# Hash attention and a gated feed forward on one core: both halves of batch 0 taken pair of heads by pair of heads, and the feed forward one stage later

## The chip, the cores and the metric

The kernel runs on 1 core of one Trainium2 chip. The metric is the device time of one execution in microseconds (us). Three runs of the kernel before gave 350.76, 349.88 and 348.50 us; their median is 349.88. The profiled execution took 349.89 us, and the span of its trace, from the first to the last instruction, is 348.1 us.

## The reference

`q`, `k` and `v` have 4 batches, 8 heads, 768 tokens and 64 dimensions; `proj` is 64 x 6. A query attends only to keys with the same six sign bits. The result, 3072 tokens of 512, goes through an RMS norm and a gated feed forward of width 1536.

```python
q_bits = (einsum('bhsd,dk->bhsk', q, proj) > 0)
k_bits = (einsum('bhsd,dk->bhsk', k, proj) > 0)
mask = q_bucket[:, :, :, None] == k_bucket[:, :, None, :]
scores = where(mask, q @ k.T / sqrt(D), -1e9)
attn = softmax(scores)
x = (attn @ v)                      # laid out as [3072, 512]
xn = x / sqrt(mean(x * x) + 1e-6) * rms_g
g = xn @ w_gate
out = (silu(g) * (xn @ w_val)) @ w_out
```

## The kernel before

**Windows, stages, slots.** The 768 queries of a batch are cut into two halves of 384, so that there are eight windows w of one batch and one half each. For one window and one head the scores come in three parts of 256 keys: two matmuls fill a tile of PSUM (`scores`, L351), and one exponential of 128 x 768 on ScalarE (ACT) empties it into `psb` (`probs`, L361). One such part is a slot, and a stage is the 24 slots of a window. Batch 0's first window alone is cut again (`UNITS`, L32): a first unit of 128 queries with 8 slots, so that its feed forward can begin early, and a second of 256 with 16. There are 192 slots in all (`SLOTS`, L34).

**Masking by bits.** The bits of a query and a key are carried as 12 extra rows of the score matmul (`KROWS` = 76). For a head, q and k are turned so that the head's dimension lies on the partitions, kept in FP32 in `T0`, multiplied with `proj` (`hash_bank`, L219), turned into signs on VectorE (`signs`, L226, the tile `bits`) and moved into rows 64 to 75 of the FP16 tile `QK`. The moves are copies on VectorE (L258) or ACT (L250, L254), or DMAs on SyncE (SP): L263 and L264 for one head, L276 for two heads (`hash_heads`, eight DMAs), L293 for two pairs (`hash_two`, eight DMAs). The values are cast into `QK` by GpSimd (POOL), L179, L194 and L211.

**Two ways to turn.** For the pairs in `BY_PE` (L38; all four of batch 0, the first two of batch 1), whole rows are loaded in one DMA (`load_rows`, L108), TensorE (PE) transposes them (`turn_pe`, L167), and VectorE or ACT copies them out (`keep`, L175). For all other pairs the load is made of blocks (`load_blocks`, L118): four DMAs for k and four for q of a pair, in pieces of 128 bytes; VectorE then transposes 32 x 32 blocks (`turn_dve`, L203).

**After the scores.** Two steps after a head's last slot `av` (L375) multiplies `psb` with `v`; after a pair of heads `attn_out` (L391 and on) adds the mean of v, divides and writes `x`. There is a single PSUM tile for `av`, and two for scores. `norm` and `turn_x` make `xnT`. The feed forward of a unit is 12 pairs of `gate` (L470, four matmuls, Tanh on ACT) and `value` (L481, four matmuls, two products on VectorE), and `project` (L495) makes the three output chunks of a window, twelve matmuls of 512 columns each. These share three banks of PSUM.

**What sets the order.** The order is written by hand: `at(s, f, ...)` places a step behind slot s, ranks order the steps of a slot, and each engine then carries out its instructions strictly in that order. `work` (L612) holds the slots at which each pair of batches 1 to 3 is loaded (k, q, v) and turned. All loads, the bits' DMAs and the outputs go through SP's queue in the order of the program; an instruction of SP waits for its tile and for one of eight semaphores. The weights `wg`, `wv` and `wo` are loaded on POOL's queue in six halves, with a cast to FP16 on the way (L543, L549). Ten buffers hold raw loads.

**Timing of the feed forward.** From window 1 on, the feed forward of a window lies in slots 8 to 24 of the stage after its attention, and its projection in the nine slots after that. The first unit's feed forward lies in slots 13 to 24, the second's in 31 to 47. The weights are issued ahead of the loop and at slots 1, 3, 6 and 8. After the last slot come the last projection of window 6, the norm, feed forward and projection of window 7.

Of the kernel before, what the change touches and what calls it, by code (L numbers as in the profile page):

```python
# [41 lines left out]
def kernel(  # L42
# [99 lines left out]
    def q_cols(w, h, i0, ni):  # L142
        b, half = divmod(w, 2)
        t = QK[b, h // 2][0:KROWS, h % 2]
        if (b, h // 2) in BY_PE:
            o = half * S + HALF + i0
            return t[:, o : o + ni]
        if b == 1:
            return t[:, 0:S].rearrange("p (c e t) -> p e c t", e=2, t=128)[:, half]
        return t[:, half * HALF + i0 : half * HALF + i0 + ni]  # L150
# [4 lines left out]
    def out_chunk(w, c):  # L155
        b, half = divmod(w, 2)
        return 2 * c + half if b < 2 else 3 * half + c
# [25 lines left out]
    def turn_head(h, n=HALF, which="kq"):  # L183

        if "k" in which:
            keep(nc.vector, 0, h, "k")
            cast_half(0, h, "k", 0)
            cast_half(0, h, "k", 1)
        if "q" in which:
            ps = keep(nc.scalar, 0, h, "q")  # L190
            nc.scalar.copy(block(0, h, 1)[:, 0:n], ps[0:64, 0:n])

    def cast_rest(h):
        nc.gpsimd.tensor_copy(block(0, h, 1)[:, 128:], t0(0, h, "q")[0:64, 128:])  # L194
# [39 lines left out]
    late = {}  # L234
# [8 lines left out]
    def hash_head(h, n=HALF, k0=None, k1=None):  # L243
# [6 lines left out]
        nc.scalar.copy(bit_rows(0, h, 1)[:, 0:n], bt[32:44, 0:n])  # L250
        for eng, t in ((k0, 0), (k1, 2)):
            src = bt[32 * t : 32 * t + 12]
            if eng is nc.scalar:
                nc.scalar.copy(bit_rows(0, h, t), src)  # L254
            elif eng is nc.sync:
                nc.sync.dma_start(out=bit_rows(0, h, t), in_=src)
            else:
                nc.vector.tensor_copy(bit_rows(0, h, t), src)  # L258
        late[h] = bt

    def late_bits(h, n=HALF):
        if n < HALF:
            nc.sync.dma_start(out=bit_rows(0, h, 1)[:, n:], in_=late[h][32:44, n:])  # L263
        nc.sync.dma_start(out=bit_rows(0, h, 3), in_=late[h][96:108])  # L264

    def hash_heads(b, hp):
        ps = hash_bank(
            [(w[:, 0:32], t0(b, 2 * hp + hh, which))
             for hh in range(2) for w, which in ((pk, "k"), (pq, "q"))]
        )  # L270
        bt = bits_tile(hp)
        signs(bt, ps)
        for hh in range(2):
            for t in range(4):
                p0 = 64 * hh + 32 * (t % 2) + 12 * (t // 2)
                nc.sync.dma_start(  # L276
                    out=bit_rows(b, 2 * hp + hh, t), in_=bt[p0 : p0 + 12]
                )
# [31 lines left out]
    def v_mean(b, hp, n, parts=(None,)):  # L310
# [7 lines left out]
        if b == 0:  # L318
            nc.scalar.mul(cvb[b % 2][:, hs, 0:65], ps, C0 / S)
        else:  # L320
            nc.vector.tensor_scalar_mul(cvb[b % 2][:, hs, 0:65], ps, C0 / S)
# [5 lines left out]
    def score_parts(n, p):  # L327

        if n == 3:
            return [(2 * p + j, 0, HALF, j, 0) for j in range(2)]  # L330
        if n == 1:
            return [(jt, 0, 128, jt // 3, 128 * (jt % 3)) for jt in range(6)]
        return [(3 * p, 0, 256, 0, 0), (3 * p + 1, 0, 256, 1, 0),
                (3 * p + 2, 0, 128, 0, 256), (3 * p + 2, 128, 128, 1, 256)]

    def prob_at(n, jt, c):

        if n == 3:
            return jt // 2, jt % 2, 128 * c
        if n == 1:  # L340
            return 0, jt // 3, 128 * (jt % 3)
        p, m = divmod(jt, 3)
        return (p, m, 128 * c) if m < 2 else (p, c, 256)

    def scores(g):
        u, h, p = SLOTS[g]
        w, c0, n = UNITS[u]
        b = w // 2
        ps = scps.tile([128, 2, 512], FP32, name="s_ps")
        for jt, i0, ni, bk, col in score_parts(n, p):  # L350
            nc.tensor.matmul(  # L351
                ps[:, bk, col : col + ni], k_cols(b, h, jt), q_cols(w, h, 128 * c0 + i0, ni),
# [4 lines left out]
    def probs(g):  # L357
        u, h, p = SLOTS[g]
        if p == 0:
            psb[u, h] = ppool.tile([128, 3, 2, HALF], FP16, name="psb")  # L360
        nc.scalar.activation(  # L361
            psb[u, h][:, p], sps.pop(g)[:, :, 0:HALF], AF.Exp, scale=ESCALE,
        )

    def av(u, h, i0, i1):
        w, c0, n = UNITS[u]
        b = w // 2
        hp, hh = divmod(h, 2)
        if hh == 0 and i0 == 0:
            ot[u, hp] = ops.tile([128, 3, 2, 66], FP32, name="o_ps")  # L370
        o = ot[u, hp]
        for i in range(i0, i1):
            c, jt = divmod(i, 6)
            p, bk, col = prob_at(n, jt, c)
            nc.tensor.matmul(  # L375
                o[:, c, hh, 0:65],
                psb[u, h][:, p, bk, col : col + 128],
# [5 lines left out]
    def attn_out(u, hp):  # L383
        w, c0, n = UNITS[u]
# [4 lines left out]
        o = ot.pop((u, hp))  # L389
        tmp = spool.tile([128, 3, 2, 66], FP32, name="otmp")  # L390
        nc.vector.tensor_add(  # L391
            tmp[:, 0:n, :, 0:65], o[:, 0:n, :, 0:65],
            cvb[b % 2][:, 2 * hp : 2 * hp + 2, 0:65].unsqueeze(1).to_broadcast([128, n, 2, 65]),
        )
        r = spool.tile([128, 3, 2, 1], FP32, name="rcp")
        nc.vector.reciprocal(r[:, 0:n], tmp[:, 0:n, :, 64:65])  # L396
# [391 lines left out]
```

## Time and profile before

| what | us |
|---|---|
| device time, median of 3 runs | 349.88 |
| device time of the profiled execution | 349.89 |
| span of its trace | 348.1 |
| PE busy | 334.9 (96%) |
| VectorE busy | 238.2 (68%) |
| ACT busy | 216.7 (62%) |
| POOL busy | 138.6 (40%) |
| first exponential, slot 0 | 15.46 |
| slot 24 / slot 48 / slot 72 | 49.86 / 83.82 / 120.86 |
| end of the last exponential | 310.22 |
| mean granted clock of PE | 0.984 |

The table of the stages in the prediction has a row for each stretch between these slots. Matmuls are pipelined, so that a busy PE can stand for one that waits within its pipeline; the distance between the starts of two matmuls says more than their durations. In the trace some groups that the change touches are these (operation, out from in, shape and count, then busy us and mean ns of one, then idle time ahead of them and what ended it):

```profile
L361 ACT ACTIVATE psb<-s_ps 128x768 f16<-128x768 f32 x192 | 151.8, 809 | 26.6 <-PE s_ps L351 26.3
L203 DVE STREAM_TRANSPOSE kT<-kL 128x384 f32<-128x384 f32 x20 | 17.7, 883 | 0.0
L175 DVE COPY kT<-t_ps 128x384 f32<-128x384 f32 x12 | 6.6, 554 | 3.3 <-PE t_ps L167 3.2
L175 ACT COPY qT<-t_ps 128x384 f32<-128x384 f32 x12 | 5.8, 479 | 3.6 <-PE t_ps L167 3.6
L179 POOL CAST QK<-kT 64x384 f16<-64x384 f32 x24 | 12.0, 501 | 9.6 <-DVE kT L175 8.7
L211 POOL CAST QK<-kT 64x768 f16<-64x768 f32 x20 | 16.4, 820 | 17.9 <-DVE kT L203 11.6
```

### The profile page before, as it was taken

Reading aid. Unit: us, or ns where it says so; the run is one execution under the profiler, and the core shown is the slowest. Engines: PE = TensorE matmul, PEld = TensorE weight load, DVE = VectorE, ACT = ScalarE, POOL = GpSimd, SP = SyncE. Lnnn points to the kernel's source line nnn. Section 1 sums busy time; section 2 is a strip of 40 time slices with the busy share of each in tenths; the row PEclk is TensorE's granted clock in tenths of the full one; section 3 lists DMA queues with packets and bytes.
Section 4 is the critical chain, followed back from the end, with each engine's and each line's share of the span. In section 5 each row is a group of like instructions: output and inputs, shape, how many; then the busy total and the mean of one; then the engine's idle time right before and its main releaser. Section 6 shows DMA issues by size and latency. Waiting matters only on the chain.

```text
span 348.1 us, 8206 instructions
## 1 busy us (share of the span) xinstructions
PE 334.9 (96%) x3172; PEld 212.5 (61%) x3172; DVE 238.2 (68%) x541; ACT 216.7 (62%) x361; POOL 138.6 (40%) x220
## 2 busy tenths in 40 slices
PE   8897998999999999999999999999999999999995
PEld 5456886666666655665566656665566656665553
DVE  3784566688678955897678866897467555675860
ACT  2587687677567755766567756775576766742321
POOL 5476544777214751286126551385111111111000
PEclk9997799999999999999999999999999999999999
DMA  7999944273399005930376008600200010001002
GB/s 216 322 237 190 246 169 89 41 130 80 61 174 149 3 6 145 185 48 5 81 179 119 3 16 200 122 2 6 73 32 1 2 60 33 2 2 74 16 3 90
DMA packets 80199, 31.42 MB, mean 90 GB/s; under 512 B 65240, under 2 KB 77216, under 8 KB 80160
## 3 DMA queue, kind: packets, MB, share of 16 engines
q1 hardware_dynamic: 76176, 26.11, 32.1%
q0 software_dynamic: 3680, 4.72, 7.9%
q8 instruction: 25, 0.41, 0.5%
q14 instruction: 14, 0.11, 0.1%
q10 hardware_dynamic: 304, 0.07, 0.1%
HBM read 28.32 MB, written 6.29 MB: 99 GB/s over the span
## 4 chain that ended last, share of the span: by engine, by line
PE 82%; DVE 11%; issue 3%; ACT 2%; POOL 2%; DVEq 0%; POOLq 0%; ACTq 0%
PE g_ps L470 17%; PE v_ps L481 17%; PE s_ps L351 16%; PE y_ps L495 15%; PE o_ps L375 9%; PE d_ps L219 3%; DVE bits L226 2%; PE x_ps L453 2%; DVE otmp L391 1%; DVE QK L258 1%; DVE xn L445 1%; DVE kT L175 1%; PE y_ps L745 1%; PE m_ps L315 1%; DVE kT L203 1%
## 5 line engine op out<-in xcount | busy, mean ns | idle before, releaser
L361 ACT ACTIVATE psb<-s_ps 128x768 f16<-128x768 f32 x192 | 151.8, 809 | 26.6 <-PE s_ps L351 26.3
L351 PE MATMUL s_ps<-QK 76*128 76x384 f16 (+2 forms) x448 | 96.6, 310 | 0.7 <-ACT psb L361 0.2
L472 ACT ACTIVATE t<-g_ps 128x384 f32<-128x384 f32 (+2 forms) x108 | 49.2, 456 | 55.7 <-PE g_ps L470 54.7
L470 PE MATMUL g_ps<-xnT,wg 128*128 128x384 f16 (+2 forms) x432 | 80.6, 309 | 1.2 <-DVE xnT L454 0.8
L481 PE MATMUL v_ps<-xnT,wv 128*128 128x384 f16 (+2 forms) x432 | 80.6, 309 | 0.7 <-DVE a L483 0.6
L495 PE MATMUL y_ps<-wo,ht 128*128 128x512 f16 x276 | 69.1, 378 | 0.3
L483 DVE SCALAR_TENSOR_TENSOR a<-t,g_ps 128x384 f32<-128x384 f32 (+2 forms) x108 | 53.9, 499 | 21.5 <-ACT t L472 19.8
L375 PEld LDWEIGHTS <-psb 128*128 128x128 f16 x1152 | 52.9, 99 | 19.3 <-issue 5.3
L484 DVE SCALAR_TENSOR_TENSOR ht<-a,v_ps 128x384 f16<-128x384 f32 (+2 forms) x108 | 55.1, 510 | 13.1 <-PE v_ps L481 3.3
L375 PE MATMUL o_ps<-vl,psb 128*128 128x65 f16 x1152 | 58.7, 195 | 2.1 <-DVE otmp L391 1.8
L399 POOL TENSOR_TENSOR x<-otmp,rcp 128x384 f32<-128x384 f32 (+2 forms) x27 | 20.4, 756 | 99.7 <-DVE rcp L396 99.5
L351 PEld LDWEIGHTS <-QK 76*128 76x128 f16 x448 | 40.0, 101 | 25.2 <-issue 1.7
L470 PEld LDWEIGHTS <-wg 128*128 128x128 f16 x432 | 39.2, 97 | 24.1 <-issue 2.9
L481 PEld LDWEIGHTS <-wv 128*128 128x128 f16 x432 | 39.3, 98 | 22.7 <-issue 1.2
L495 PEld LDWEIGHTS <-ht 128*128 128x128 f16 x276 | 24.1, 97 | 20.9 <-issue 0.5
L502 ACT COPY ysb<-y_ps 128x512 f32<-128x512 f32 x23 | 13.5, 586 | 29.4 <-PE y_ps L495 29.1
L391 DVE TENSOR_TENSOR otmp<-o_ps,cvb 128x390 f32<-128x390 f32 (+2 forms) x36 | 18.5, 513 | 17.1 <-PE o_ps L375 14.7
L454 DVE TENSOR_TENSOR xnT<-x_ps,gcol 128x512 f16<-128x512 f16 x24 | 16.6, 691 | 12.7 <-PE x_ps L453 12.6
L211 POOL CAST QK<-kT 64x768 f16<-64x768 f32 x20 | 16.4, 820 | 17.9 <-DVE kT L203 11.6
L226 DVE TENSOR_SCALAR bits<-d_ps,thr,scl 128x384 f16<-128x384 f32 x20 | 13.2, 677 | 12.9 <-PE d_ps L219 12.7
L211 POOL CAST QK<-qT 64x768 f16<-64x768 f32 x20 | 16.4, 820 | 11.9 <-DVE qT L203 11.0
L413 POOL TENSOR_TENSOR sq<-x 128x384 f32<-128x384 f32 (+1 forms) x24 | 19.2, 800 | 1.9
(74 smaller groups left out, 281.6 us busy)
## 6 DMA issues: line engine op xcount, KB each, us to landing
vL<-in_v_dram SPq DMA_DIRECT2D x16, 384.0 KB
out_dram<-ysb SPq DMA_DIRECT2D x23, 256.0 KB
kL<-in_k_dram SPq DMA_DIRECT2D x40, 96.0 KB
qL<-in_q_dram SPq DMA_DIRECT2D x40, 96.0 KB
kL<-in_k_dram SPq DMA_DIRECT2D x5, 384.0 KB
qL<-in_q_dram SPq DMA_DIRECT2D x5, 384.0 KB
wg<-in_moe_w_gate_dram POOLq DMA_DIRECT2D x2, 768.0 KB, 10.6
wv<-in_moe_w_val_dram POOLq DMA_DIRECT2D x2, 768.0 KB, 8.9
```

The source lines that it names most:

```text
L211: nc.gpsimd.tensor_copy(QK[b, hp][0:64, hh, o : o + S], T0[b, hp, which][64 * hh : 64 * hh + 64, :])
L351: nc.tensor.matmul(ps[:, bk, col : col + ni], k_cols(b, h, jt), q_cols(w, h, 128 * c0 + i0, ni), start=True, stop=True,)
L361: nc.scalar.activation(psb[u, h][:, p], sps.pop(g)[:, :, 0:HALF], AF.Exp, scale=ESCALE,)
L375: nc.tensor.matmul(o[:, c, hh, 0:65], psb[u, h][:, p, bk, col : col + 128], vls[b % 2][:, h, v_chunk(b, h, jt), 0:65], start=(hh == 0 and ...
L391: nc.vector.tensor_add(tmp[:, 0:n, :, 0:65], o[:, 0:n, :, 0:65], cvb[b % 2][:, 2 * hp : 2 * hp + 2, 0:65].unsqueeze(1).to_broadcast([128, ...
L399: eng.tensor_mul(xd.rearrange("p c (h d) -> p c h d", h=2), tmp[:, 0:n, :, 0:64], r[:, 0:n].to_broadcast([128, n, 2, 64]),)
L470: nc.tensor.matmul(g, wg[:, kt, fs], xnT[w][:, kt, cs], start=(kt == 0), stop=(kt == 3))
L472: nc.scalar.activation(t, g, AF.Tanh, scale=0.5)
L481: nc.tensor.matmul(vv, wv[:, kt, fs], xnT[w][:, kt, cs], start=(kt == 0), stop=(kt == 3))
L483: nc.vector.scalar_tensor_tensor(out=a, in0=t, scalar=1.0, in1=g, op0=ALU.add, op1=ALU.mult)
L484: nc.vector.scalar_tensor_tensor(out=ht[w][:, ft, cs], in0=a, scalar=0.5, in1=vv, op0=ALU.mult, op1=ALU.mult)
L495: nc.tensor.matmul(y, ht[w][:, ft, c * 128 : (c + 1) * 128], wo[:, ft, :], start=(ft == 0), stop=(ft == NF - 1),)
```

## The change

The units are gone. The 48 slots of batch 0 go through the pairs of heads; for each pair first the one half's two heads, then the other half's. Batches 1 to 3 keep their order.

- `BY_PE` holds batch 0 alone: the first two pairs of batch 1 are loaded in blocks and turned by VectorE, and their bits come from `hash_two`. All loads of batch 1 are given earlier slots (from slot 9 on instead of 21).
- The heads of batch 0 are prepared later: only heads 0 and 1 ahead of the loop; heads 2 and 3 in slots 0 to 4, heads 4 and 5 in slots 6 to 13, heads 6 and 7 in slots 16 to 23. The bits of heads 4 to 7 are moved by `hash_heads`, eight DMAs on SP for a pair.
- The six weight loads are issued at slots 4, 11, 17, 23, 29 and 35.
- The feed forward of window w lies in slots 24w + 48 to 24w + 64 and its projection in the nine after that, so it comes one stage later than before. Those of windows 6 and 7 lie behind the last slot.
- `v_mean` of batch 0 leaves ACT for VectorE; `AHEAD`, the slot from which an exponential is placed behind the early steps of the slot before, is 3 instead of 24.

```diff
-UNITS = [(0, 0, 1), (0, 1, 2)] + [(w, 0, 3) for w in range(1, 8)]
-BASE = [0, 8] + [24 * w for w in range(1, 8)]
-SLOTS = [(u, h, p) for u, (_, _, n) in enumerate(UNITS) for h in range(H) for p in range(n)]
+SLOTS = [(w, 2 * hp + hh, p) for hp in range(H // 2) for w in range(2)
+         for hh in range(2) for p in range(3)]
+SLOTS += [(w, h, p) for w in range(2, 8) for h in range(H) for p in range(3)]
+LAST = {(w, h): g for g, (w, h, p) in enumerate(SLOTS) if p == 2}
-BY_PE = [(0, hp) for hp in range(4)] + [(1, 0), (1, 1)]
+BY_PE = [(0, hp) for hp in range(4)]
...
+    def hash_heads(hp):
...
+        for hh, t in [(0, 0), (0, 2), (0, 1), (1, 0), (1, 2), (1, 1), (0, 3), (1, 3)]:
+            p0 = 64 * hh + 32 * (t % 2) + 12 * (t // 2)
+            nc.sync.dma_start(out=bit_rows(0, 2 * hp + hh, t), in_=bt[p0 : p0 + 12])
...
+    turn_head(nc.vector, 0, "k")
+    casts(0, 0)
+    turn_head(nc.scalar, 0, "q", True)
     columns_of_proj()
+    turn_head(nc.vector, 1, "k")
+    casts(0, 2)
+    hash_head(0, (nc.vector, nc.scalar, nc.vector, nc.sync))
+    turn_head(nc.scalar, 1, "q", True)
     scores(0)
+    hash_head(1, (nc.vector, nc.scalar, nc.vector, nc.sync))
+    v_prep(0, 0)
...
+    for hp, turns in ((1, (0, 1, 2, 3)), (2, (6, 8, 10, 12)), (3, (16, 18, 20, 22))):
+        for i, s in enumerate(turns):
+            at(s, keep_pair, hp, i, nc.scalar if hp == 1 and i % 2 else nc.vector)
+            at(s + (hp > 1), casts, hp, i)
+    at(2, hash_head, 2, (nc.vector, nc.vector, nc.vector, nc.sync))
+    at(4, hash_head, 3, (nc.sync, nc.sync, nc.sync, nc.sync))
+    at(13, hash_heads, 2)
+    at(23, hash_heads, 3)
...
+    for i, s in enumerate((4, 11)):
+        at(s, load_w, (wg, wv)[i], (moe_w_gate, moe_w_val)[i], 0, 768)
+    for i, s in enumerate((17, 23)):
+        at(s, load_w, (wg, wv)[i], (moe_w_gate, moe_w_val)[i], 768, 1536)
+    at(29, load_wo, 0, 6)
+    at(35, load_wo, 6, 12)
...
-        (1, 0): ((21, 22, 23), (28, 29, 30, 31)), (1, 1): ((24, 25, 26), (33, 34, 35, 36)),
-        (1, 2): ((27, 30, 33), (35, 37, 39, 40)), (1, 3): ((32, 35, 39), (41, 43, 45, 47)),
+        (1, 0): ((9, 11, 14), (24, 26, 28, 30)), (1, 1): ((15, 18, 20), (31, 32, 34, 35)),
+        (1, 2): ((22, 25, 30), (37, 38, 40, 41)), (1, 3): ((28, 32, 36), (43, 47, 49, 51)),
...
+        s0 = 24 * w + 48
         seen = set()
         for ft in range(NF):
-            for f, s in ((g_step, s0 + (ns * ft) // NF),
-                         (v_step, s0 + (2 * ns * ft + ns) // (2 * NF))):
-                at(s, f, u, ft, rank=4 if s in seen else 2)
+            for f, s in ((g_step, s0 + 16 * ft // NF), (v_step, s0 + (32 * ft + 16) // (2 * NF))):
+                at(s, f, w, ft, rank=4 if s in seen else 2)
                 seen.add(s)
+        for i in range(9 if w < 7 else 6):
             c, j = divmod(i, 3)
+            at(s0 + 16 + i, project, w, c, 4 * j, 4 * j + 4, rank=1 if i == 8 else 3)
-    AHEAD = 24
+    AHEAD = 3
```

More of the change, by code (lines that the diff above doesn't have):

```diff
@@ L156, in out_chunk @@
         b, half = divmod(w, 2)
-        return 2 * c + half if b < 2 else 3 * half + c
+        return 2 * c + half if b == 0 else 3 * half + c
     def turn_pe(b, h, which):
@@ L181, in cast_half, with turn_head @@
         )
[L183 to L194, printed above, removed]
+    def turn_head(eng, h, which, direct=False):
+        ps = keep(eng, 0, h, which)
+        if direct:
+            nc.scalar.copy(block(0, h, 1), ps[0:64])
     def turn_dve(b, hp, which, part):
@@ L726 @@
             f()
-    for s in range(NS, NS + 13):
+    for s in range(NS, 24 * 10):
         for _, _, f in steps(s):
             f()
-    project(6, 0, 0, NF)
-    norm(8)
-    project(6, 1, 0, NF)
-    for c in range(3):
-        turn_x(8, c)
-        project(6, 2, 4 * c, 4 * c + 4)
-    for ft in range(NF):
-        value(8, ft, gate(8, ft))
-    for c in range(2):
-        project(7, c, 0, NF)
     y = bank("y_ps")
```

282 lines of the change are left out of this document (83 added, 199 removed).

## The prediction

> **What bounds the kernel now.** I read the busy rows, then the span cut at the exponentials that open each stage of 24 steps, then the costliest groups, then the DMA issues in order of time. One slot is one exponential (L361, 192 of them); slot 0 starts at 15.46 us, slot 48 at 83.82, slot 72 at 120.86, and slot 191 ends at 310.22. Columns below: stretch, its length, busy us of PE, PEld, DVE, ACT, POOL, then granted clock, DMA share, GB/s.
>
> ```profile
> 0.00:15.46 15.46, 12.68 (x98) 8.16 (x102) 7.52 (x35) 5.56 (x12) 7.69 (x29) 1.00 0.88 270
> 15.46:49.86 34.40, 31.28 (x407) 24.51 (x407) 22.71 (x59) 26.94 (x56) 21.32 (x41) 0.85 1.08 228
> 49.86:83.82 33.96, 31.78 (x350) 22.97 (x350) 24.81 (x60) 24.46 (x42) 22.02 (x35) 1.00 0.39 72
> 83.82:120.86 37.04, 36.26 (x361) 22.78 (x358) 28.98 (x64) 24.41 (x39) 15.75 (x22) 1.00 0.57 104
> 120.86:310.22 189.36, 189.07 (x1748) 114.89 (x1747) 133.66 (x283) 125.35 (x195) 70.81 (x95) 1.00 0.28 61
> 310.22:348.10 37.88, 33.79 (x223) 19.20 (x221) 20.58 (x44) 9.96 (x21) 1.04 (x2) 0.99 0.12 43
> ```
>
> From 120.86 us on PE is the bound: the starts of its matmuls lie 162 ns apart at 384 columns, 215 ns at 512 and 32 ns in attention times values, and these alone fill the 189.36 us. The first 84 us are something else: before 50 us the DMA engines are full (share 1.08), and the clock fell to half from 29.8 to 40.0 us.
>
> ```profile
> PEclk9997799999999999999999999999999999999999
> DMA  7999944273399005930376008600200010001002
> ```
>
> SyncE's DMA queue matters for what follows, so its issues in order of time (start, duration, what):
>
> ```profile
> 55.47 2.75 SPq L118 DMA_DIRECT2D kL<-in_k_dram  x4
> 58.32 2.65 SPq L118 DMA_DIRECT2D qL<-in_q_dram  x4
> 63.33 6.20 SPq L276 DMA_DIRECT2D QK<-bits  x8
> 73.77 0.40 SPq L108 DMA_DIRECT2D vL<-in_v_dram  x1
> 88.13 6.26 SPq L293 DMA_DIRECT2D QK<-bits  x8
> ```
>
> Issuing costs SP itself 0.69 us for each quarter of a block load (2.75 for four), 0.77 for a bits move, 0.45 for a V load. Its eight completion semaphores go round, so no more than eight DMAs are out.
>
> **Sums.** The profiled execution spans 348.1 us and is timed 349.89, so 1.8 us is added to a span; the median is 349.88.
>
> *What is moved off the first 48 slots.* All of window 0's feed forward (96 matmuls x 162 ns = 15.6 us) and its first projection chunk (12 x 215 = 2.6) leave them. The chunk goes to slots 48 to 72: 37.04 + 2.6 = 39.6 us. Slots 72 to 192 then hold the same counts as before, one feed forward and one projection later: 189.4. The end gets one feed forward more, beside which the last norm is hidden: 37.9 + 15.7 = 53.6 (twelve pairs of gate and value, 1.3 us each; ACT's 0.49 and VectorE's 1.1 a pair lie beside that, and the last norm's 6 us on VectorE beside the next projection, 0 to 2 if the banks hold PE up, taken as 0). So the span is T48 + 282.6, where T48 is the start of slot 48, and the change breaks even at T48 = 65.5 instead of 83.8.
>
> *What is removed outright.* 24 FP32 transposes (starts 115 ns apart) are 2.8 us of PE; two hash banks of batch 1, at 5.7 us for eight, 1.4; the small matmuls of the first unit hold the same columns, but 160 matmuls fewer at the fixed 3 ns that 162 and 215 ns leave, 0.5. All of it lies before slot 48, so it counts only if PE ends last there. Batch 1's first two pairs now take eight VectorE transposes (880 ns) for four copies of 554 ns, and four fewer ACT copies; the means of batch 0 (four of 287 ns) go to VectorE. VectorE has no feed forward before slot 48, so these are hidden: 0 of the sum, at most 5 if they ended last.
>
> *T48 if nothing but PE and ACT mattered.* Scores 96 x 165 ns = 15.8, attention times values 288 x 32 = 9.2, transposes 36 x 115 = 4.1, four banks 2.8, means 1.4: 33 us of PE; ACT 48 exponentials 0.69 apart: 33. Waiting on each other I take 0.8 a slot (back to back 0.69; 1.17 in the 16 slots to 49.86 us, half of them at half clock). Slot 0 moves up behind the second head's bit copy, from 15.46 to 12.4, since heads 2 and 3 no longer go ahead of it on ACT. So 12.4 + 48 x 0.8 = 51.
>
> *T48 by SP's queue.* This is the term I believe in. In program order SP issues, after head 3's signs (slot 4, about 18.5 us): four bits moves, eight block quarters, eight bits (heads 4 and 5), V, eight quarters, V, four quarters, eight bits (heads 6 and 7), eight quarters, V, four quarters, V, and then the bits of batch 1's first two pairs, of which scores(48) needs the first four. Before, batch 1's first pairs were six single issues. That is 24 bits moves x 0.77 + 32 quarters x 0.69 + 4 V x 0.45 = 42.4 us; a bits move lands 1.4 us after its issue. T48 is not under 18.5 + 42.4 + 1.4 = 62.3. PE is in order, so scores(24), scores(36) and scores(48), each waiting for bits, hold everything behind them.
>
> *T48 with the weights beside it.* Before, block loads (128-byte records) first moved at 57 us, after the last weight record at 45. Now all six weight loads fall among them. Counting the trace's DMA records: alone, SP's ring moves 1310 block records per us or 251 of 1536 bytes. While weights stream, the two rings take turns record by record: 85 weight records per us (134 ns) to 81 of SP's (78 ns) at 13 to 18 us, 107 (96 ns) to 103 at 38 to 42, and each engine starts a weight record every 190 ns. With 13 ns block records a turn is about 132 ns, so SP's ring gets 121 records per us instead of 1310: a block load of 3072 nearly stands still for the 4.3 us of a wg or wv half and the 4.8 us of a wo half. By POOL's order (casts 0.55 us, V casts and products 0.83, issue 0.85, data 2.5 us later) I place the weights at 21.5, 28.2, 33.8 and 39.7, and wo, behind casts of batch 1, near 46.5 and 54. In what is left, k and q of pair (1,0) finish near 37, its followers k(1,1) 46, q(1,1) 52, k(1,2) 60. The bits queued behind them make slot 24 about 38 (unhindered 31.6), VectorE's transposes of (1,1) hold slots 31 and 34, and slot 36 comes at 61 (unhindered 41). The last of heads 6 and 7's bits goes out near 62, then 9.15 us of loads, 3.05 of bits and 1.4 of landing: T48 = 76. With head 3's signs 2 us either way and other gaps I get 73 to 80. Between the ends 51, 62.3 and 80 I take 76, as the record counts are the nearest rows.
>
> The DMA page of the Trainium skill ("DMA: Bandwidth & Descriptors", Queues, rings and completion order) says that an engine drains a packet of typically 9 to 17 descriptors from one ring before it switches. The strict turns of one record, every 190 ns, disagree.
>
> *Clock.* The new waits of 5 to 8 us leave PE idle. The half-clock stretch before took 10.24 us; within slots 24 to 48 a slot of 0.69 us of PE becomes 1.4, still mostly under the DMA waits, but a half clock just after slot 48 costs up to 3. I take 1.
>
> The sum: 76 + 282.6 + 1 + 1.8 = 361 us, 3% slower.
>
> The clock-gate page ("TensorE: Matmul & The Clock Gate", Part 1) has the clock halve after an idle window of about 3.4 us. By it each of those waits would do so; only the 10.24 us stretch here speaks to that.
>
> **Rivals.**
> 1. *The weights don't hold SP's ring*: block records go many to a turn. T48 is SP's own 62.3, and the time 62.3 + 282.6 + 1.8 = 347, 1% faster at best. For it: no row shows 128-byte records beside weights. Against it: two sizes both showed turns of one record. The skill's rule of packets (same page; its table of SWDGE and HWDGE puts a packet at up to 4096 bytes) would lead here. By turns of 32 records of 128 bytes the ring would keep over 900 a us.
> 2. *The order on SP doesn't bind*: SP runs ahead of its schedule or bits come in time. Then T48 is 51 and the time 335, 4% faster; it decides wherever T48 falls below 62. Against it: the 0.69 and 0.77 us are SP's own time, whoever waits.
> 3. *Half way*: gaps between the weights fall well, T48 63 to 69, 347 to 353.
> 4. *The clock as well*: every wait costs a half-clock stretch that isn't covered, and FFN's start at slot 48 is slow: 365 to 370.
> 5. *The start isn't early*: slot 0 stays at 15.46; all of SP's chain moves 2 to 3 us, 363, inside the forecast's range.
>
> **How the numbers follow.** Within 1% (346.4 to 353.4) is about what a measurement can't tell from no change. Forecast, T48 73 to 80 (357 to 366, rival 5 in it): 0.66. Rival 1: 0.15, by its own spread of 2 us half below 346.4. Rival 2: 0.07. Rival 3: 0.07, of it 0.05 within. Rival 4: 0.05. Faster 0.08 + 0.07 = 0.15; same 0.07 + 0.05 = 0.12; slower 0.66 + 0.05 + 0.02 = 0.73. The range leaves out rival 2 and the far ends: 344 to 369. The forecast's own range is 357 to 366.
>
> **What would show it.** In the changed profile: slot 0 near 12.4; PE waiting at slots 24, 36 and 48 with a bits DMA named; SP's issues without a gap from slot 4 to 48; the block loads longer from first issue to last landing (5.4 us before) than 10; the clock halved somewhere between 30 and 80 us; then slots 72 to 192 in 189 us and an end of 53.6. The forecast is wrong if T48 is below 66, or if slots 48 to 192 or the end are other than these rows, which would mean that a VectorE turn or a bank ends last there.

## The result, and the profile after

The changed kernel takes 412.6 us (median of four runs, 409.23 to 413.75) against 349.88: a ratio of 1.178, interval 1.170 to 1.186. The profiled execution took 413.75 us with a span of 411.9 us, 63.8 us more than the span before. The forecast was 361 us, a span of 359.6: the sign is right, the size is not, and the time lies far outside the range.

In the listing of the changed kernel the exponential is L319, the score matmuls L309, gate L403, value L413, the two products of a gate and value pair on VectorE L415 and L416, the norm L346 to L384, the turn of its result L391, block loads L120, row loads L110, `hash_heads` L259 and `hash_two` L274.

First the span cut at the start of slots 0, 24, 48, 72, 168 and at the end of slot 191, with the columns of the table in the prediction (stretch, length, busy us of PE, PEld, DVE, ACT, POOL, then granted clock, DMA share, GB/s):

```profile
0.00:12.24 12.24, 8.71 (x63) 5.63 (x64) 5.34 (x30) 3.99 (x7) 5.33 (x24) 1.00 0.83 269
12.24:40.73 28.49, 20.33 (x236) 13.31 (x239) 12.27 (x27) 18.80 (x27) 23.37 (x39) 0.90 0.97 171
40.73:86.68 45.95, 26.55 (x239) 15.40 (x236) 22.17 (x43) 18.39 (x24) 20.03 (x25) 0.65 0.82 141
86.68:131.24 44.56, 41.51 (x374) 24.97 (x372) 32.06 (x66) 24.68 (x39) 16.56 (x22) 0.93 0.39 76
131.24:309.62 178.38, 164.49 (x1414) 97.55 (x1413) 110.40 (x232) 101.15 (x156) 65.02 (x88) 0.92 0.28 60
309.62:350.80 41.18, 37.88 (x335) 23.07 (x334) 21.74 (x49) 25.16 (x39) 5.90 (x8) 0.96 0.05 17
350.80:411.90 61.10, 52.84 (x328) 29.77 (x324) 32.36 (x66) 15.91 (x32) 1.16 (x3) 0.97 0.10 35
```

PE does fill 36.26 of 37.04 us in a stage before; now it is idle for some 3 us of each stage of 44.5, and the clock is below 1 in every stage. The profile's rows of clock and DMA over 40 slices say where:

```profile
PEclk9997565968999969996999889996999899989999
DMA  7799996750173174215604280110001000100102
```

Before, one stretch showed a clock below 9 tenths. Now the clock is at half for most of 35 to 90 us (stretches of 17.1, 17.1 and 6.8 us), and then there is a dip in each stage, some 44 us apart. The list of what PE waited for (us in total, times, longest) names both kinds:

```profile
PE s_ps L309 <- DMA QK<-bits: 19.9, 2, 13.1
PE v_ps L413 <- DVE a L415: 13.9, 4, 4.4
PE m_ps L296 <- DVE a L415: 10.3, 3, 3.7
PE x_ps L391 <- DVE xn L384: 5.2, 1, 5.2
```

The first is the opening: bits at slots 24 and 36, as forecast. The second and third were not forecast: seven waits for a product of the feed forward on VectorE, of 2.9 to 4.4 us, one in each of the six stages and one behind the last slot. The fourth, for window 0's norm, stands in front of slot 48. The account of the spans, in us, cut at the starts of slots 48, 72 and 191 (the forecast's 189.4 and 53.6 are counted from the end of slot 191, 0.8 later; E1 is the first experiment below; its slots 48 to 72 hold no projection yet, and its end holds one more):

| stretch | before | forecast | after | E1 |
|---|---|---|---|---|
| start of slot 48 | 83.8 | 76 | 86.7 | 87.8 |
| slots 48 to 72 | 37.0 | 39.6 | 44.6 | 38.3 |
| slot 72 to slot 191 | 188.5 | 188.6 | 218.8 | 189.9 |
| from slot 191 on | 38.7 | 54.4 | 61.9 | 63.7 |
| clock | | 1 | | |
| sum | 348.1 | 359.6 | 411.9 | 379.7 |

Of the 52 us that the forecast lacks, 10.7 are at slot 48, 35 in the six stages from there to slot 191, and 7.5 behind it (less the 1 set aside for the clock).

**What happens in a stage.** The timeline of the changed kernel in the third stage, from slot 72 on (start, duration, engine, line, operation, and in brackets the idle time before it with what ended it):

```profile
138.68 0.81 PE L403 MATMUL g_ps<-xnT,wg 128*128 128x384 f16 x4
...
139.57 0.56 DVE L346 TENSOR_TENSOR otmp<-o_ps,cvb 128x390 f32<-128x390 f32 x1
139.66 0.81 PE L413 MATMUL v_ps<-xnT,wv 128*128 128x384 f16 x4
...
140.38 0.56 DVE L354 TENSOR_TENSOR x<-otmp,rcp 128x384 f32<-128x384 f32 x1
...
141.74 0.17 DVE L375 TENSOR_REDUCE ss<-ssp 128x3 f32<-128x12 f32 x1
...
141.99 0.20 POOL L377 TENSOR_SCALAR ms<-ss 128x3 f32<-128x3 f32 x1 [4.94 <-DVE ss L375]
142.27 0.86 POOL L381 TENSOR_TENSOR rstd<-ms,mhalf 128x3 f32<-128x3 f32 x1
143.16 1.28 DVE L384 TENSOR_SCALAR xn<-x,rstd 128x512 f16<-128x512 f32 x3 [1.26 <-POOL rstd L381]
144.36 0.55 DVE L415 SCALAR_TENSOR_TENSOR a<-t,g_ps 128x384 f32<-128x384 f32 x1
144.96 1.44 PE L413 MATMUL v_ps<-xnT,wv 128*128 128x384 f16 x4 [3.23 <-DVE a L415]
```

The Tanh of the gate at 138.68 had ended at 140.02, so that its product `a` could have run then. But VectorE is in order, and the norm of the window that has just ended stands ahead of them: from 139.57 to 144.4, of which 1.26 us VectorE itself waits for POOL. So `a` comes at 144.36; that gate, its value and the next gate fill all three banks meanwhile, and the next value's matmuls wait 3.23 us for one. Then the clock is at half for 6.8 us: the four value matmuls at 144.96 take 1.44 us instead of 0.81. Three stretches of this stage, cut around that place:

```profile
131.24:140.50 9.26, 9.26 (x85) 5.06 (x84) 4.78 (x10) 5.45 (x9) 5.46 (x8) 1.00 0.11 42
140.50:149.00 8.50, 5.28 (x36) 2.95 (x35) 4.64 (x15) 2.06 (x5) 1.06 (x2) 0.72 0.29 51
149.00:175.60 26.60, 26.60 (x237) 16.34 (x236) 19.35 (x35) 17.70 (x28) 12.21 (x16) 0.96 0.51 93
```

The time is lost in the middle one and in the first 2 us of the third, where the half clock ends: 3.2 us of waiting and up to 3.4 us by the 6.8 at half clock, up to 6.6 together. This stage has become 6.4 us longer (44.36 against 37.94). The same norm stood in the kernel before, 127.2 to 132.1 us in its third stage, and cost nothing:

```profile
120.86:131.00 10.14, 10.14 (x100) 5.33 (x99) 6.06 (x18) 5.90 (x9) 5.97 (x9) 1.00 0.04 9
131.00:139.00 8.00, 8.00 (x69) 4.75 (x67) 4.89 (x10) 4.47 (x8) 1.01 (x2) 1.00 0.60 148
```

There the slots beside the norm hold the projection, which reads nothing that VectorE is about to make. The change moves the feed forward from slots 8 to 24 of a stage to slots 0 to 16, onto the norm; the projection goes where the feed forward was.

**What happens in the opening.** SP's queue of the changed kernel (start, duration of all, what, how many):

```profile
31.59 7.23 SPq L259 DMA_DIRECT2D QK<-bits  x8
...
39.53 7.60 SPq L120 DMA_DIRECT2D kL<-in_k_dram  x4
47.23 3.47 SPq L120 DMA_DIRECT2D qL<-in_q_dram  x4
...
51.48 8.12 SPq L120 DMA_DIRECT2D kL<-in_k_dram  x4
59.70 7.33 SPq L259 DMA_DIRECT2D QK<-bits  x8
```

The bits that slot 36 needs go out at 59.70 behind four quarters that took 8.12 us to issue, not 2.75: SP itself was held up while weights streamed. By what, the views do not name; it was not the eight completion semaphores, since those that the quarters issued at 52.10 and 55.63 use had been free since 48.5 and 49.4. Counting the trace's DMA records, the two rings take turns one by one here too, with 128-byte records: 252 weight records (138 ns each) to 239 block records (26 ns) from 30 to 32 us, 350 (99 ns) to 341 (26 ns) from 54 to 56. In the second of these stretches the starts of both kinds repeat every 80 to 90 ns, in the first every 120 to 130, as single turns would and packets of many records would not.

In front of slot 48 two things end together: the bits that it needs land between 81.8 and 83.6 us, and PE's wait of 5.2 us for window 0's norm ends at 83.78.

### The profile page after: what moved, and what is told of

The parts are those of the page before. It is cut to its first block, busy times and chain, and to the rows that moved or that the text cites. A ratio compares the mean times of both kernels' runs of the same rounds, so it can differ in the third digit from the quotient of the medians.

```text
span 411.9 us, 7717 instructions
## 1 busy us (share of the span) xinstructions
PE 352.3 (86%) x2972; PEld 209.7 (51%) x2972; DVE 236.4 (57%) x512; ACT 208.1 (51%) x322; POOL 137.3 (33%) x207
## 4 chain that ended last, share of the span: by engine, by line
PE 75%; DVE 12%; DMA 4%; POOL 3%; issue 2%; SPq 1%; ACT 1%; POOLq 0%; DVEq 0%; ACTq 0%
PE s_ps L309 15%; PE v_ps L413 15%; PE y_ps L427 14%; PE g_ps L403 14%; PE o_ps L331 8%; PE d_ps L210 4%; DMA QK<-bits 2%; DVE xn L384 2%; DMA qL<-in_q_dram 2%; DVE sq L361 2%; PE x_ps L391 2%; POOL rstd L381 1%; DVE otmp L346 1%; DVE x L354 1%; DVE a L415 1%
## 5 line engine op out<-in xcount | busy, mean ns | idle before, releaser
L319 ACT ACTIVATE psb<-s_ps 128x768 f16<-128x768 f32 x192 | 151.0, 809 | 59.8 <-PE s_ps L309 55.6
L309 PE MATMUL s_ps<-QK 76*128 76x384 f16 x384 | 102.5, 352 | 23.5 <-DMA QK<-bits 19.9
L405 ACT ACTIVATE t<-g_ps 128x384 f32<-128x384 f32 x96 | 47.1, 490 | 108.2 <-PE g_ps L403 108.0
L413 PE MATMUL v_ps<-xnT,wv 128*128 128x384 f16 x384 | 84.0, 344 | 13.9 <-DVE a L415 13.9
L403 PE MATMUL g_ps<-xnT,wg 128*128 128x384 f16 x384 | 83.5, 342 | 0.3
L415 DVE SCALAR_TENSOR_TENSOR a<-t,g_ps 128x384 f32<-128x384 f32 x96 | 52.6, 548 | 45.8 <-ACT t L405 44.1
L427 PE MATMUL y_ps<-wo,ht 128*128 128x512 f16 x276 | 68.7, 378 | 0.0
L354 POOL TENSOR_TENSOR x<-otmp,rcp 128x384 f32<-128x384 f32 x24 | 19.9, 827 | 138.5 <-DVE rcp L351 138.1
L416 DVE SCALAR_TENSOR_TENSOR ht<-a,v_ps 128x384 f16<-128x384 f32 x96 | 53.2, 554 | 13.3 <-PE v_ps L413 4.9
L413 PEld LDWEIGHTS <-wv 128*128 128x128 f16 x384 | 37.7, 101 | 38.1 <-issue 17.4
L309 PEld LDWEIGHTS <-QK 76*128 76x128 f16 x384 | 33.1, 103 | 41.0 <-issue 28.8
L403 PEld LDWEIGHTS <-wg 128*128 128x128 f16 x384 | 37.5, 102 | 27.3 <-issue 7.0
L346 DVE TENSOR_TENSOR otmp<-o_ps,cvb 128x390 f32<-128x390 f32 x32 | 17.7, 554 | 23.8 <-PE o_ps L331 23.8
L434 ACT COPY ysb<-y_ps 128x512 f32<-128x512 f32 x23 | 13.5, 585 | 22.1 <-PE y_ps L427 19.2
L194 DVE STREAM_TRANSPOSE qT<-qL 128x384 f32<-128x384 f32 x24 | 20.1, 880 | 5.3 <-DMA qL<-in_q_dram 5.3
```

The lines of the kernel that those rows point to most:

```text
L309: nc.tensor.matmul(ps[:, j, 0:HALF], k_cols(w // 2, h, 2 * p + j), q_cols(w, h), start=True, stop=True,)
L319: nc.scalar.activation(psb[w, h][:, p], sps.pop(g)[:, :, 0:HALF], AF.Exp, scale=ESCALE,)
L346: nc.vector.tensor_add(tmp[:, :, :, 0:65], o[:, :, :, 0:65], cvb[b % 2][:, 2 * hp : 2 * hp + 2, 0:65].unsqueeze(1).to_broadcast([128, 3, 2 ...
L354: eng.tensor_mul(xd.rearrange("p c (h d) -> p c h d", h=2), tmp[:, :, :, 0:64], r.to_broadcast([128, 3, 2, 64]),)
L403: nc.tensor.matmul(g, wg[:, kt, fs], xnT[w][:, kt], start=(kt == 0), stop=(kt == 3))
L405: nc.scalar.activation(t, g, AF.Tanh, scale=0.5)
```

## The experiments

Two questions. *Stages*: theory, the feed forward lies on the norm's chain on VectorE; rival, the later feed forward costs in itself (buffers, ACT, the clock). *Opening*: theory, weights and block loads taking turns set slots 24, 36 and 48; rival, something else in the order (VectorE's turns, window 0's norm) sets slot 48 whatever the DMAs do. Each experiment edits the changed kernel. Ratios are against the kernel before, and the numbers of slots are the starts of their exponentials.

**E1: the feed forward and projection 8 slots later**, back on the place within a stage that they had before.

```diff
-        s0 = 24 * w + 48
+        s0 = 24 * w + 56
...
```

> Every feed forward and projection 8 slots later than in the changed kernel (slots 24w + 56 on), so that projections, which need nothing of VectorE, lie beside the norm again. Theory: the 44 us of each stage come from the norm's chain on VectorE ahead of the first products, with PE idle 3 to 6 us and then at half clock. Then slots 72 to 192 take 189 to 193 us (219.6 before), the part behind the last exponential's start about 61, since one projection more lies there, and the time is about 371. Rival: the stages are long because VectorE and the banks are short of time wherever the feed forward lies; then slots 72 to 192 stay over 210 and the time over 395. Slot 48 stays at 86 to 87 in both.

Measured: 379.89 us, ratio 1.086 (1.081 to 1.092), 33 us less than the changed kernel. All seven waits are gone (one of 3.25 us for a turn on VectorE, at 97.6, comes in slots 48 to 72), and from slot 72 to 191 the clock stays at 1.00 with PE full:

```profile
126.10:315.90 189.80, 188.66 (x1739) 113.91 (x1737) 133.36 (x282) 125.45 (x194) 70.65 (x95) 1.00 0.28 60
315.90:379.70 63.80, 58.41 (x368) 32.54 (x364) 34.90 (x70) 18.50 (x37) 2.70 (x4) 1.00 0.11 38
```

The counts of work are the same, VectorE's busy time too; only the place is another. The stages are explained. The total is 9 us above the expectation of 371, mostly because that was summed wrongly: its own parts (slot 48 at 86 to 87, 189 to 193 and 61, with the forecast's 39.6 for slots 48 to 72) come to about 377. Of the rest, slot 48 is 1 us late, and the end took 63.7 us. That is the forecast's 54.4, one more projection (7.7) that now lies behind the last slot, and 1.6 for one wait.

**E2: feed forward left where the change puts it, the norm split.** The multiplication `xn` is issued two slots behind the rest of the norm (for window 0 in the same slot), so that VectorE does not wait for POOL with products queued behind it.

```diff
         nc.gpsimd.tensor_tensor(out=rstd, in0=ms, in1=mhalf, op=ALU.pow)
+        rstds[w] = rstd
+
+    def norm_x(w):
+        rstd = rstds[w]
         xn[w] = npool.tile([128, 3, DMODEL], FP16, name="xn")
...
+        at(LAST[w, 7] + (3 if w == 0 else 5), norm_x, w, rank=5)
```

> The feed forward where the change puts it, but the three multiplications of the norm placed two slots behind its sums, so that VectorE goes through products while POOL makes the root. If the idle wait for POOL (1.3 us) tips it, the stages fall from 44 us to 39 to 40 and the time to about 385. If the whole chain of about 4.4 us of VectorE does, the wait only gets shorter: stages of 41 to 43, time 395 to 408.

Measured: 383.86 us, a single run and so without an interval; it agrees with the first of the two expectations (about 385). PE's waits for VectorE's products are short now:

```profile
PE v_ps L419 <- DVE a L421: 3.8, 4, 1.8
PE m_ps L296 <- DVE a L421: 2.6, 3, 1.2
```

24.2 us of them have become 6.4, the longest is 1.8 instead of 4.4, and no half clock is left between slot 72 and the last slot; the stages take 39.3 to 40.7 us. So two edits that share only the norm's place against the feed forward take the loss away. The remaining 1 to 2 us a stage are the rest of the norm, still ahead of the products.

**E3: E1 with the weights after the block loads**, to see whether they hold the opening.

```diff
-    for i, s in enumerate((4, 11)):
+    for i, s in enumerate((37, 40)):
...
-    for i, s in enumerate((17, 23)):
+    for i, s in enumerate((43, 46)):
...
-    at(29, load_wo, 0, 6)
-    at(35, load_wo, 6, 12)
+    at(49, load_wo, 0, 6)
+    at(53, load_wo, 6, 12)
```

> As the first of these runs, and the six weight loads at slots 37, 40, 43, 46, 49 and 53 in place of 4 to 35. Theory: weights take turns with block loads record by record, and the bits queued behind are late by that. Then slot 24 falls from 40.7 us to 32 to 35, slot 36 from 67.5 to 47 to 52, slot 48 from 86.7 to 62 to 70, and the time to about 350. Rival: SP's own issue and its eight open DMAs set the pace, weights or not: slot 48 stays over 78 and the time over 362.

Measured: 376.3 us, 1.078 (1.073 to 1.082). Slot 24 came at 33.7 (E1: 42.1) and slot 36 at 51.2 (68.6): the weights cost these slots 8 and 17 us. Slot 48 came at 81.7, and with the time it lies where the rival put it. The weights now run beside batch 1's last loads:

```profile
65.36 5.96 SPq L110 DMA_DIRECT2D vL<-in_v_dram  x1
71.41 9.38 SPq L274 DMA_DIRECT2D QK<-bits  x8
```

A V load that took 0.45 us to issue takes 5.96, and the bits that slot 48 needs leave behind it; PE waits 10.1 us for them. So the weights do hold the earlier slots, against the rival, but moving them moves the wait.

**E4: E1 with heads 4 to 7 hashed singly and their bits copied by VectorE**, so that these bits do not stand in SP's queue.

```diff
-    at(13, hash_heads, 2)
-    at(23, hash_heads, 3)
+    for h, s in ((4, 9), (5, 13), (6, 19), (7, 23)):
+        at(s, hash_head, h, (nc.vector, nc.vector, nc.vector, nc.vector))
```

> As the first of these runs, with the bits of heads 4 to 7 moved by 16 copies of VectorE instead of 16 DMAs on SP (head by head: two hash banks and two sign passes more, 2.8 us of PE and VectorE). Theory: the waits of 6.8 us at slot 24 and 13.1 at slot 36 are bits standing behind block loads; they go, and loads of batch 1's pair (1,1) are next (VectorE's turns at slots 31 to 34). Slot 36 falls from 67.5 to 50 to 56 us, slot 48 to 70 to 76, the time to 355 to 361. Rival: the block loads themselves are the limit and only change who waits: slot 48 stays over 80, the time over 364.

Measured: 372.06 us, 1.062 (1.056 to 1.069). Slot 24 at 39.3, slot 36 at 53.1 as expected, slot 48 at 80.1 and the time where the rival put them: PE now waits 9.5 us at 67.8 for VectorE, which itself waits 8.8 us for a block load of k.

**E5: E3 and E4 together.**

> The third and fourth runs together: feed forward 8 slots later, weights at slots 37 to 53, bits of heads 4 to 7 by VectorE. Theory: the two are parts of one queue (weights hold block loads, block loads hold bits), so with both gone SP's chain is about 25 us long and no weights stand beside it. Slot 36 at 42 to 47 us, slot 48 at 55 to 62, time 347 to 354. Rival: something else holds slots 42 to 48 (the norm of window 0, VectorE's turns); then slot 48 stays over 70 and the time over 362.

Measured: 366.22 us, 1.046 (1.042 to 1.051). Slots 24, 36 and 48 at 38.4, 51.7 and 70.5. No bits DMA of the opening is waited for, and still it is not the 55 to 62 expected: PE waits 6.5 us for window 0's norm in front of slot 48, and the slots between 24 and 36 take 1.1 us each. The rival's two marks are met.

**E6: E5 with the feed forward 4 slots later instead of 8, and window 0's turn into `x_ps` three slots later**, behind slot 48.

```diff
-        s0 = 24 * w + 56
+        s0 = 24 * w + 52
...
-            at(LAST[w, 7] + (4 if w == 0 else 7) + c, turn_x, w, c, rank=1)
+            at(LAST[w, 7] + 7 + c, turn_x, w, c, rank=1)
```

> As the run of both, with the feed forward only 4 slots later than in the changed kernel (24w + 52) and window 0's turns for the feed forward at slots 48 to 50 instead of 45 to 47. Theory: a projection still covers the norm at steps 2 and 3, PE has work again 4 slots earlier, and the 5 us wait of PE for the norm of window 0 goes. Slot 48 at 52 to 57, stages 37 to 39, time 341 to 347, under the kernel before. Rival: 4 slots of projection are too few and the wait comes back in part (stages over 40), time over 352.

Measured: 368.05 us, 1.051 (1.046 to 1.055). The rival's time. Slot 48 came at 63.9, 6.7 us earlier than in E5, and slots 48 to 72 took 45.7 us instead of 39.8. Some 4.7 us of that is work that now lies there: four of window 0's nine projection steps (16 matmuls at 215 ns) and its turn (12 transposes, 0.11 us apart). And part of the wait has crossed the mark: PE waits 3.2 us for window 0's norm at 67.5, and 2.7 at 78.5 for VectorE, which had window 1's norm before that. Slots 72 to 191 took 192.4 us instead of 189.8, so four slots of projection cover all but some 3 us of the norm in these stages.

**E7: E1 with the first two pairs of batch 1 turned by rows on PE**, as in the kernel before: their loads are long records again, and VectorE has eight copies in place of eight longer turns (in the kernel before ACT made four of them). Their bits go through `hash_heads`.

```diff
-BY_PE = [(0, hp) for hp in range(4)]
+BY_PE = [(0, hp) for hp in range(4)] + [(1, 0), (1, 1)]
...
+        if by_pe:
+            for i, s in enumerate(turns):
+                h, which = 2 * hp + i // 2, "kq"[i % 2]
+                at(s, keep, nc.vector, b, h, which)
+                for par in range(2):
+                    at(s + 1, cast_half, b, h, which, par)
+            at(turns[3] + 1, hash_heads, hp, b)
```

> The first of these runs, with batch 1's first two pairs loaded in rows and turned by PE as in the kernel before (four row loads in place of 16 quarters, 24 transposes more on PE, 16 bits moves instead of 8). Theory: the block loads are what holds the bits, so slot 24 falls from 42 us to 32 to 35, slot 36 from 68.6 to 48 to 54, slot 48 from 87.8 to 66 to 74, time 358 to 366. Rival: the weights alone hold SP's ring, whatever stands in it; slot 36 stays over 60 and the time over 370.

Measured: 369.22 us, 1.057 (1.051 to 1.062). Slots 24, 36 and 48 at 34.8, 54.8 and 73.2, with waits of 7.5 us for bits and 5.2 for window 0's norm. Slot 48 lies in what was expected; slot 36 and the time just miss. Loading these pairs in blocks and turning them on VectorE thus costs E1 some 11 us (379.89 against 369.22), all of it ahead of slot 48, which comes 14.6 us earlier in the two profiled runs. The edit changes loads, turns and bits together, so it does not say which of them costs it.

**E8: E7 with the weights late as in E3.**

> Feed forward 8 slots later, batch 1's first two pairs by rows and PE, and the weights at slots 37 to 53. Theory: with neither block loads nor weights ahead of the bits, slots 24 and 36 start without a DMA wait (32 to 34 and 44 to 48 us), slot 48 at 60 to 66, time 353 to 359: the best of these arrangements, and still not under the kernel before, since nothing of the feed forward is done by slot 48. Rival: with the DMA waits gone the prologue runs at 0.8 us a slot, slot 48 at 51 to 54, time under 347.

Measured: 373.0 us (four runs, 370.21 to 378.96; the trace is of the one at 375.68), 1.066 (1.056 to 1.076), clear above the expected 353 to 359. Slots 24 and 36 at 33.6 and 45.9 as expected, some 0.95 us a slot from 36 to 42 without a DMA wait; then one wait of 19.3 us and slot 48 at 76.5, far later than expected:

```profile
PE x_ps L394 <- DVE xn L387: 20.9, 2, 19.3
```

The norm itself is not that long. VectorE stood 11.5 us, until 68.69, before a turn of k blocks of batch 1's last pair. (The view names a DMA of bits that landed at the same moment; the last of the k records landed at 68.5.) Those records were taking turns with the weights: 161 of them to 228 weight records from 64 to 66 us.

**E9: E1 with the weights early**, the other end.

```diff
-    for i, s in enumerate((4, 11)):
+    for i, s in enumerate((0, 1)):
...
-    for i, s in enumerate((17, 23)):
+    for i, s in enumerate((2, 3)):
...
-    at(29, load_wo, 0, 6)
-    at(35, load_wo, 6, 12)
+    at(6, load_wo, 0, 6)
+    at(8, load_wo, 6, 12)
```

> Feed forward 8 slots later, block loads as in the changed kernel, the weights at slots 0, 1, 2, 3, 6 and 8, where the kernel before had most of them. Theory: the six loads then stand as one run of about 27 us from 16 to 20 us on, in front of the first block loads: slot 24 is later than 42.1 us (46 to 52), but slot 36 comes with SP's own pace behind it (64 to 68) and slot 48 at 80 to 86, time 372 to 379. Rival: it is SP's own issuing that sets slot 24 and 36, not the weights; then slot 24 stays within 2 us of 42.

Measured: 380.78 us, 1.089 (1.083 to 1.096), no better than E1. Slot 24 at 49.2 and slot 36 at 66.9 as expected; slot 48, at 87.1, and the time are just outside. SP's queue:

```profile
22.33 10.50 SPq L120 DMA_DIRECT2D kL<-in_k_dram  x4
32.92 11.62 SPq L120 DMA_DIRECT2D qL<-in_q_dram  x4
```

All weights landed between 23.6 and 44.3 us, and just so long SP needs for eight quarters: 22.1 us instead of 5.4.

**E10: E7 with the weights early**, so that they meet rows and not blocks.

> The kernel with feed forward and projection 8 slots later and batch 1's first two pairs turned by rows (369.22 us), now with the weights at slots 0, 1, 2, 3, 6 and 8, so that they run before the first block loads and, by the record turns, neither stands in the other's way. Theory (the opening is set by weights and block records taking turns): slot 24 at 33 to 36, slot 36 at 46 to 50, slot 48 at 56 to 64, the time 350 to 357. Rival (another wait is next, VectorE's norm of window 0 and the turns of the later pairs): slot 48 at 70 or later, the time 364 or more.

Measured: 367.94 us, 1.053 (1.050 to 1.056): the rival. Slots 24, 36 and 48 at 35.1, 54.6 and 73.2, as in E7 within 0.3 us. Rows do not escape: four row loads queued at 34 to 37 us take turns with `wo` (211 weight records to 200 row records from 42 to 44 us), and the quarters and bits behind them wait:

```profile
36.55 13.30 SPq L120 DMA_DIRECT2D kL<-in_k_dram  x4
```

**E11: E10 with window 0's turn into `x_ps` behind slot 48, and earlier turns of batch 1's last pair.**

```diff
-        (1, 2): ((22, 25, 30), (37, 38, 40, 41)), (1, 3): ((28, 32, 36), (43, 47, 49, 51)),
+        (1, 2): ((22, 25, 30), (37, 38, 40, 41)), (1, 3): ((28, 32, 36), (43, 45, 46, 47)),
...
-            at(LAST[w, 7] + (4 if w == 0 else 7) + c, turn_x, w, c, rank=1)
+            at(LAST[w, 7] + 7 + c, turn_x, w, c, rank=1)
```

> The kernel before in this job (rows, weights early, feed forward 8 slots later) with window 0's turn into x_ps at slots 48 to 50 and the turns of the last pair of the first four at slots 43, 45, 46 and 47. If the wait that is left in front of slot 48 is window 0's norm on VectorE, it is now covered by the units that follow it: 4 to 8 us less than that kernel, 343 to 350, level with or below the 349.9 of the kernel before. If a transfer is what is late there, no more than 1 us less.

Measured: 369.54 us, 1.056 (1.053 to 1.060), no gain. (The expectation's range is a slip: 4 to 8 us less than 367.94 would be 360 to 364.) Slot 48 came 4.5 us earlier, at 68.7, and slots 48 to 72, with the same feed forward in them, took 44.9 us instead of 38.7; some 1.3 us of that is window 0's turn. PE now waits 4.7 us at 77.7 for `xnT` of window 0, which on VectorE stands behind two turns that had waited 2.9 us for a load of q, and 2.5 us at 87.1 for window 1's norm; the clock is at half for 13.7 us from 67.2. So the norm of window 0 no longer held slot 48, but a transfer was late too, the expectation's second case.

**E12: E10 with the bits of heads 4 to 7 copied by VectorE, as in E4.**

> The kernel with feed forward and projection 8 slots later, batch 1's first two pairs turned by rows and the weights at slots 0 to 8 (367.94 us), now with heads 4 to 7 hashed singly and their bits copied by VectorE, so that they no longer stand on SP behind block quarters (13.30 us for four at 36.6 in that kernel) and behind row loads that take turns with the last weights up to 49 us. Theory (slot 36 there is late by SP's order, and what is late at slot 48 follows from slot 36): slot 36 at 44 to 49 instead of 54.6, slot 48 at 60 to 67, the time 354 to 361. Rival (slot 48 is held by batch 1's bits and window 0's norm whenever slot 36 comes, since the DMA engines are full up to 49 us): slot 36 as in the theory, but slot 48 at 69 or later and the time 364 or more.

Measured: 365.41 us, 1.045 (1.040 to 1.049), the shortest time of these runs, though not clear of E5's 366.22, and with slot 48 at 72.4 the rival's. But neither had slot 36 right: 55.2, not 44 to 49, and slot 24 is 41.6 instead of 35.1. The stretches from slot 0 to 24 and on to 36:

```profile
12.40:41.60 29.20, 23.87 (x249) 14.54 (x249) 19.97 (x41) 19.14 (x27) 21.17 (x35) 0.94 1.12 247
41.60:55.20 13.60, 12.06 (x142) 8.05 (x141) 9.97 (x21) 9.29 (x12) 11.24 (x20) 1.00 1.08 177
```

In these 43 us no wait of PE is longer than 2.0 us, none is for bits, and the slots take 1.2 us each. The DMA engines are full to 55 us; VectorE is busy 73% of the second stretch, POOL 83%. Then 5.9 us go for window 0's norm again. What sets these 1.2 us is not settled.

## Why the prediction was right and wrong

**The step that failed** is "Slots 72 to 192 then hold the same counts as before, one feed forward and one projection later: 189.4". The counts are the same, and the time is 219.6 us, because the feed forward also moved within its stage, onto the norm. The prediction had the chain in its hand ("the last norm's 6 us on VectorE beside the next projection, 0 to 2 if the banks hold PE up, taken as 0") and put it beside the projection, where it stood before and no longer stands. It named the cover of that one norm and did not ask what covers the others; only its last sentence, on what would show it wrong, has a VectorE turn or a bank ending last. Of the lacking 52 us this step made 30 in slots 72 to 192, and the same mechanism most of the 5 in slots 48 to 72 and of the 7.5 at the end, where PE waits 4.4 us at 362.4 with half clock behind it. E1 gives 189.9 for the same stretch, and E2, with the feed forward left in place, 39.3 to 40.7 a stage: shown by two edits.

**Much of its size came from the clock.** In the third stage a wait of 3.2 us costs up to 6.6, since the clock then falls to half for 6.8 us in which PE is full. The seven waits add up to 24.2 us. The seven stretches at half clock, four of 6.8 us and three of 3.4, add up to 37.6, of which at most half, 18.8, is lost. The prediction took 1 us for the clock in all. It is rival 4's mechanism, at a place that rival did not look at, and it priced 4 to 9 us in all. The Trainium skill ("TensorE: Matmul & The Clock Gate", Part 1) has the clock halve after an idle window of about 3.4 us. The seven waits, of 2.9 to 4.4 us, agree with it nearly; that one of 2.95 us is enough is a little less than the page's figure.

**The opening was right in kind, too small in size.** Slot 0 came at 12.24 (12.4 said), so rival 5 is out. PE waits at slots 24 and 36 with the bits DMA named, the turns are one record each with 128-byte records too, and the block loads are held: rival 1 is out, and with it the Trainium skill's packets of 9 to 17 descriptors ("DMA: Bandwidth & Descriptors", Queues, rings and completion order) for the case that had no row before. Rivals 2 and 3, with a slot 48 at 51 and 63 to 69, are out too. Slot 24 is 40.7 (38 said), slot 36 67.4 (61), slot 48 86.7 (76). The mis-sized term is SP's 0.69 us a quarter, "SP's own time, whoever waits": it is not that beside weights. Four quarters took up to 8.12 us there, and the bits queued behind them inherit it: the last of heads 6 and 7's are out at 67.0 (62 said), and the loads between them and the bits of slot 48 take 12.0 us (9.15 said). And the last wait in front of slot 48 is not for bits but 5.2 us for window 0's norm on VectorE (x_ps, in the list of waits), which the ledger did not have; the bits had landed only just before, so that the two are about equally late. The sign of the forecast is not luck: E1, without the loss in the stages, is still 30 us slower than the kernel before.

**"The change breaks even at T48 = 65.5"** treated slot 48 as a mark behind which nothing changes. E11 shows that it is not: with slot 48 4.5 us earlier than in E10, the next 24 slots took 6.3 us more, of which 1.3 is work that was moved there; E6 shows it in part. What VectorE still owes at that place, window 0's norm and turns that wait for loads, is waited for either ahead of the mark or behind it.

**Where the expected gain went.** 18.2 us of PE work left the first 48 slots, and slot 48 came 2.9 us later than before. In E5, E7, E10 and E12 it came 11 to 13 us earlier than before, with the whole feed forward of another window waiting at the end. E1's end is 25.0 us longer than before and its slots 48 to 191 take 2.6 us more; to pay for that, slot 48 would have to come at 56.2 (83.8 less 27.6), and no run came there (the earliest is E6's 63.9). So the pairwise order is not worth it in any version tried, and the kernel before remains the fastest. Still open: what holds the first 36 slots at 1.1 to 1.2 us each once no bits are waited for (E5, E12), and what in the transfers holds SP's issues beside weights.

## What to carry to other kernels

When a block of work is moved by a whole stage, check also where it lands within the stage: list for each in-order engine what stands at that place already, and whether the moved work needs that engine to free its buffers. Here a chain of small operations across two engines was hidden only beside work that needed nothing of either engine: the projection, not the gated products, belongs beside the norm. And price a wait of PE of about 3 us or more above its length if PE is full behind it: with up to half of the 3.4 or 6.8 us at half clock, the seven here cost at most 1.4 to 2.1 times their length.

## What the hardware showed that was not expected

- **A queue's issue time is not a constant.** Four block quarters cost SP 2.7 us with no weights beside them (at 70.4 us in the changed kernel), up to 8.1 beside weights, 10.5 to 13.3 in E9 and E10.
- **The clock falls by stretches of 3.4 us.** Half-clock stretches in these traces last 3.4, 6.8, 10.2, 13.7, 17.1 or 23.9 us. One long wait is not needed: in E12 the clock was half for 3.4 us from 33.1 on. In the 3.4 us before that PE was busy for 1.66 us, and its longest wait was 1.4; in the 3.4 us before those it was busy for 2.04, and the clock stayed full.
- **VectorE slows beside POOL.** In the changed kernel window 0's norm ran beside POOL's casts, and the same operations took 1.5 to 3.3 times as long as in the later stages (0.56 us for `x`, 0.29 for a square):

```profile
78.97 0.83 DVE L354 TENSOR_TENSOR x<-otmp,rcp 128x384 f32<-128x384 f32 x1
79.84 0.80 DVE L361 SCALAR_TENSOR_TENSOR sq<-x 128x128 f32<-128x128 f32 x1
...
80.56 0.95 DVE L361 SCALAR_TENSOR_TENSOR sq<-x 128x128 f32<-128x128 f32 x1
...
81.45 0.28 DVE L361 SCALAR_TENSOR_TENSOR sq<-x 128x128 f32<-128x128 f32 x1
```

The third square falls into a time in which POOL has ended its casts, and takes 0.28 us again. `otmp` at 78.15, with one of its two inputs in PSUM, also ran beside a cast and took its usual 0.56 us. The Trainium skill ("GPSIMD Engine Reference", Specifications) says that the two engines share their way into SBUF, with contention where a VectorE instruction has two inputs there. The slowed operations have two, and the trace agrees.
